# The first of equal maxima by a small bf16 product, one slot later, and weight conversions placed anew

## The chip, the cores and the metric

The kernel runs on one core of a Trainium2 chip. The metric is device time in microseconds for one execution, the median of eight: 1227.68 us (1223.66 to 1229.91). Five engines work side by side, each through its own instructions in order: TensorE (PE; its weight loads are PEld), VectorE (DVE), ScalarE (ACT), GpSimd (POOL) and SyncE (SP), whose queue issues most of the transfers.

## The reference: clustered attention, then a gated feed-forward layer

```python
# q, k, v: (4, 8, 768, 64) f32; centroids (8, 16, 64) f32
q_assign = argmax(q_n @ c_n.T)        # cluster of each query, first of equal maxima
k_assign = argmax(k_n @ c_n.T)        # cluster of each key
mask = q_assign[:, :, :, None] == k_assign[:, :, None, :]
scores = where(mask, q @ k.T / 8, -1e9)
scores = scores - max(scores)
attn = exp(scores) / (sum(exp(scores)) + 1e-9)
x = (attn @ v) -> (3072, 512)         # heads side by side
h = x @ w_in                          # w_in (512, 2048), float64
out = (h * erf(softplus(h))) @ w_out  # w_out (2048, 512), float64
```

A query attends only to the keys of its own cluster. Where no key has it, all scores are equal.

## The kernel before

**Pairs and units.** A pair `p` is two heads of one batch; there are 16, four to a batch. For each pair there are 12 units: two halves of 384 queries times six blocks `j` of 128 keys. For one unit, `scores` multiplies k and q in f32 (`products`, one product for each head `e`) and adds a bf16 product of `km` and `qm`; ScalarE takes the exponential into `pr`; `accumulate` lets POOL sum `pr` over the blocks; `attend` multiplies `pr` with v into `av`. After six units `divide` sums over partitions (`psum`, TensorE), takes the reciprocal by a logarithm and an exponential (`inv`, ScalarE), refines it (`den`, VectorE) and writes the quotient `xT` (VectorE). `divide` is in two parts: the first issues `psum` and `inv`, the second the rest.

**Routing of a pair.** `qm` and `km` (bf16, in `lows`) hold for each head the other head's vectors and, in 32 more rows, one-hot clusters: 1 for a query's own cluster, and for a key 0 at its cluster and at most -2^60 elsewhere. Their product is 0 within a cluster and hugely negative without. `route(p)` makes them, with a `yield` between its steps: (1) load and transposition of q and k on VectorE; (2) the product with the centroids (`psim`) on TensorE and the casts of q's vectors on ScalarE (`vectors("q")`); (3) transposition out of PSUM (`sims`), first maximum over 16 clusters (`mx`) and comparison with it; (4) the casts of k's vectors on ScalarE; (5) the choice of the first of equal maxima: the comparison's 0 or 1 times a descending `rank`, a second maximum `mr`, then two comparisons (equality for the queries' 64 partitions, a difference for the keys') into `hot`, and its transposition `hotT`; (6) the conversion of `hotT` into `qm` and `km`: two pieces on VectorE, four and then two on ScalarE. `own` zeroes the rows of the other head.

**Maxima of a pair.** `shift(p)` is 24 products `sm` of `qm` and `km` with VectorE's maximum over each (`nmx`); after each half `nm`, a small transposition `pn` on TensorE, a copy `nmT` on ScalarE, and six transfers that put the maxima into a row of `qm`. Two `sm` make a step; the half's end (`nm`) and `pn` are steps too, 14 in all. `aside(p)` is `route` and then `shift`: 20 steps.

**Weights.** They come as float64 and are converted to f32 by integer work: per tile of 128x512, ScalarE's `split` (two instructions), three steps on VectorE (A: a lower bound, B: shift and mask, C: the sign and the rest) and one addition on POOL after C. C also issues the next tile's split, B issues a fetch on SP's queue. 32 tiles are 96 steps; `prepare(n)` runs `n` of them. Tiles wait in the space of `w_out` and in two halves of `a_s`.

**Order.** Batch 0 is a loop over 48 slots, one unit each, kept in the written order up to slot 44 (`FIRST` is 45). `plan` has one line for each slot `r` of a pair (r0 to r11): steps of the pair's own maxima, steps of the next pair's `aside` before and after the unit's scores, and conversion steps. The first part of `divide` runs at r2 and r8, before the steps "after"; the second part at r3 and r9. In slots 44 and 45 no conversions run. From slot 45 on, `pump` mixes in the feed-forward stream: `hp` (x times `w_in`), the gate on ScalarE (Softplus and Erf into `a_s`, each with a load of its function table) and POOL, and `po` (times `w_out`). From batch 1 on, units go in twos, five places to each, 30 to a pair; `ASIDE` lists the places at which a step of the next pair's `aside` runs, and a planner that works with its own estimates of cost is free to move instructions from there on, also ahead of earlier ones where nothing binds them.

**PSUM.** `ps_s` has two double buffers for `sc`. `ps_x` has four buffers that `psim`, `sm`, `pn`, `av`, `psum`, `hp` and `po` share: a product that starts in a buffer waits until the last reader of the tile before has done.

Most rows of the profile name line 58, since one helper records the instructions; they are told apart by the tiles. The functions in question:

Of the kernel before, what the change touches and what calls it, by code (L numbers as in the profile page):

```python
# [8 lines left out]
F32 = mybir.dt.float32  # L9
BF16 = mybir.dt.bfloat16  # L10
U32 = mybir.dt.uint32
I32 = mybir.dt.int32
ALU = mybir.AluOpType
ACT = mybir.ActivationFunctionType
AX = mybir.AxisListType
PSUM = bass.MemoryType.PSUM

P = 128
B, H, S, D = 4, 8, 768, 64
C = 16  # L20
NJ = S // P
Q = 32
NB = S // Q
HW = S // 2
# [11 lines left out]
BIG = 2.0**60  # L36
# [5 lines left out]
SLOTS = 5  # L42


ASIDE = (*range(5), 6, *range(8, 8 + 2 * NJ), 10 + 2 * NJ, 12 + 2 * NJ)
REST = 3
FIRST = 2 * NJ * HP - 3

# [18 lines left out]
def kernel(  # L67
# [20 lines left out]
    const = pool("const", 1)  # L88
# [3 lines left out]
    routep = pool("routep", 1)  # L92
# [7 lines left out]
    ps_x = pool("ps_x", 4, space=PSUM)  # L100
# [1 line left out]
    ident = const.tile([P, P], F32, name="ident")  # L102
    identb = const.tile([P, P], BF16, name="identb")
    minus = const.tile([P, D], F32, name="minus")
    rank = const.tile([P, C], F32, name="rank")
    ccT = const.tile([P, HP, 2 * C], F32, name="ccT")
    w_in = const.tile([P, DM // P, DFF], F32, name="w_in")
    w_out = const.tile([P, NFT, DM], F32, name="w_out")
# [52 lines left out]
            ge.memset(t["k"][e * D + SH : e * D + SH + 1, e], 1.0)  # L161
    for t in prs:
        ge.memset(t[:, :, HW : HW + 2], EPS)

# [105 lines left out]
    def route(p):  # L272
        st = pairs[p]
        low = lows[p % 2]
        for e in range(2 if p > 1 else 0):
            r = e * D + SH
            nc.sync.dma_start(out=low["q"][r : r + 1, e], in_=low["q"][r + 1 : r + 2, e])
        for nm in "qk":
            raw = rowp.tile([P, S], F32, name=nm + "T")
            ve.transpose(out=raw, in_=st.pop(nm).rearrange("p n t -> p (n t)"))  # L280
            st[nm + "T"], st[nm + "m"] = raw, low[nm]
        load_qk(p + 1)
        yield

        psim = ps_x.tile([P, HW], F32, name="psim", tag="x")
        for g in range(4):
            te.matmul(
                psim[2 * C * g : 2 * C * (g + 1)], lhsT=ccT[:, p % HP],
                rhs=st["qk"[g // 2] + "T"][:, (g % 2) * HW : (g % 2 + 1) * HW],
                start=True, stop=True,  # L290
            )

        def vectors(nm):
            for e in range(2):
                ae.copy(
                    out=low[nm][(1 - e) * D : (2 - e) * D, e], in_=st[nm + "T"][e * D : (e + 1) * D]
                )

        vectors("q")
        yield  # L300

        sims = routep.tile([P, HW], F32, name="sims")
        ve.transpose(out=sims, in_=psim)
        n = HW // C
        sim = sims.rearrange("p (g c) -> p g c", c=C)
        mx = routep.tile([P, n], F32, name="mx")
        ve.reduce_max(out=mx, in_=sim, axis=AX.X)
        ve.tensor_tensor(
            out=sim, in0=sim, in1=mx.unsqueeze(2).to_broadcast([P, n, C]), op=ALU.is_equal
        )  # L310
        yield
        vectors("k")
        yield

        ve.tensor_tensor(
            out=sim, in0=sim, in1=rank.unsqueeze(1).to_broadcast([P, n, C]), op=ALU.mult
        )
        mr = routep.tile([P, n], F32, name="mr")
        ve.reduce_max(out=mr, in_=sim, axis=AX.X)

        hot = routep.tile([P, HW], BF16, name="hot")
        for r, op in ((slice(0, D), ALU.is_equal), (slice(D, P), ALU.subtract)):
            ve.tensor_tensor(
                out=hot[r].rearrange("p (g c) -> p g c", c=C), in0=sim[r],
                in1=mr[r].unsqueeze(2).to_broadcast([D, n, C]), op=op,
            )
        hotT = routep.tile([P, HW], BF16, name="hotT")
        ve.transpose(out=hotT, in_=hot)
        yield
        late = []  # L330
        for half in range(2):
            cols = slice(half * HW, (half + 1) * HW)
            for e in range(2):
                r = slice(e * D, e * D + Q)
                g = slice(half * Q, (half + 1) * Q)
                if half == 0:
                    ve.tensor_scalar_mul(out=low["q"][r, e, cols], in0=hotT[g], scalar1=own[g, e : e + 1])
                else:
                    late.append((low["q"][r, e, cols], hotT[g], own[g, e : e + 1]))
                g = slice(D + half * Q, D + (half + 1) * Q)  # L340
                ae.copy(out=low["k"][r, e, cols], in_=hotT[g])
        for dst, src, scale in late:
            ae.activation(out=dst, in_=src, func=ACT.Copy, scale=scale)
        yield


# [249 lines left out]
    def aside(p):  # L596
# [3 lines left out]


    plan = (
        (1, 0, 1, 1), (1, 0, 2, 0), (1, 0, 2, 0), (1, 0, 1, 0), (0, 0, 0, 0), (0, 0, 2, 0),
        (0, 0, 2, 1), (0, 0, 2, 1), (0, 1, 0, 3), (0, 0, 0, 3), (0, 0, 2, 1), (0, 0, 1, 2),
    )
    ready = {0: aside(0)}
    part = iter(())
# [1 line left out]
    def advance(p, n):  # L609
        for _ in range(n):  # L610
            next(ready[p])
# [9 lines left out]
        )  # L621
    ve.tensor_copy(out=identb, in_=ident)
    ve.memset(minus, -1.0)
    for c in range(C):
        ve.memset(rank[0:D, c : c + 1], float(C - c))
    ve.tensor_scalar_mul(out=rank[D:P], in0=rank[0:D], scalar1=BIG)
    ve.memset(alleps, S * EPS)
    for t in maxima:
        ve.memset(t, FLOOR)
# [6 lines left out]
    advance(0, 1)  # L636
    products(0)
    products(1)
    advance(0, 4)
    prepare(2)  # L640
    advance(0, NJ + 1)
    prepare(1)
# [98 lines left out]
```

## Time and profile before

| | |
|---|---|
| median of eight executions | 1227.68 us |
| the profiled execution | 1226.05 us |
| its span, first to last instruction | 1224.2 us |
| busy: PE / DVE / ACT / POOL | 1157.0 / 540.0 / 567.8 / 464.8 us |
| mean granted TensorE clock | 0.987 |
| slots of batch 0, about | 31 to 195 us |
| transfers | 42.95 MB |

A row of a group has the engine, the operation, output and inputs, sizes and count; then busy us, mean ns of one, idle time before, and what ended that. In rows in order of time the first two numbers are start and duration in us. TensorE's f32 products appear as two records each. `w_out` in a VectorE or ScalarE row of batch 0 is mostly a weight tile in conversion, since the tiles wait in that space.

### The profile page before, as it was taken

The numbers are of one execution on the slowest core, as the hardware profiler recorded it, in microseconds if no ns is written. First come the engines' busy times: TensorE is split into PE (matmuls) and PEld (weight loads), VectorE is DVE, ScalarE is ACT, GpSimd is POOL, SyncE is SP. The second block draws the span as 40 slices with busy tenths as digits, with TensorE's granted clock in tenths as the row PEclk, the third lists the DMA queues.
The fourth block names the chain that finished last, engine by engine and source line by source line (L and its number), as shares of the span: only waits on it lengthen the run. The fifth ranks groups of instructions, "written<-read, shape, count | busy, mean of one in ns | idle before, by whom it ended". The sixth has DMA issues, their size and how long they took to land.

```text
span 1224.2 us, 13359 instructions
## 1 busy us (share of the span) xinstructions
PE 1157.0 (95%) x4897; PEld 617.5 (50%) x4897; DVE 540.0 (44%) x999; ACT 567.8 (46%) x675; POOL 464.8 (38%) x462
## 2 busy tenths in 40 slices
PE   4888879989999999999999999999999999999998
PEld 1222235554454445565455445556456456576663
DVE  6889885674444345334344345334435112011121
ACT  3656556658352637165364445356263254132222
POOL 2467764357332344144343244235234343030200
PEclk9999999899999999999999999999999999999999
DMA  7344323132020202010020201002000000000000
GB/s 134 80 102 103 83 83 84 42 104 40 9 48 9 48 1 40 9 35 13 14 44 1 48 10 27 22 10 39 9 22 1 9 9 1 17 1 17 1 18 18
DMA packets 140753, 42.95 MB, mean 35 GB/s; under 512 B 133520, under 2 KB 133520, under 8 KB 140688
## 3 DMA queue, kind: packets, MB, share of 16 engines
q1 hardware_dynamic: 137552, 41.70, 15.2%
q10 hardware_dynamic: 3136, 0.39, 0.3%
q8 instruction: 39, 0.64, 0.2%
q14 instruction: 26, 0.21, 0.1%
HBM read 35.68 MB, written 6.29 MB: 34 GB/s over the span
## 4 chain that ended last, share of the span: by engine, by line
PE 74%; DVE 11%; issue 7%; ACT 6%; DMA 2%; POOL 0%; SPq 0%; ACTq 0%; DVEq 0%
PE po L58 25%; PE hp L58 24%; PE sc L58 12%; PE av L58 7%; PE sm L58 4%; DVE nmx L58 3%; ACT L58 2%; DVE w_out L58 2%; DVE den L58 1%; ACT inv L58 1%; PE psim L58 1%; DVE sims L58 1%; PE psum L58 1%; ACT km L58 1%; ACT pr L58 1%
## 5 line engine op out<-in xcount | busy, mean ns | idle before, releaser
L58 PE MATMUL hp<-xT,w_in 128*128 128x256 f32 x1536 | 382.7, 386 | 3.3 <-DVE xT L58 2.4
L58 PE MATMUL po<-w_out,g 128*128 128x512 f32 x768 | 367.8, 597 | 0.6 <-DVE den L58 0.6
L58 POOL TENSOR_TENSOR acc<-acc,pr 128x384 f32<-128x384 f32 x256 | 239.6, 967 | 316.0 <-ACT pr L58 315.8
L58 PEld LDWEIGHTS hp<-xT,w_in 128*128 128x128 f32 x1536 | 286.1, 191 | 121.5 <-issue 79.8
L58 DVE TENSOR_REDUCE nmx<-sm 128x1 f32<-128x384 f32 x384 | 195.2, 550 | 145.2 <-PE sm L58 144.4
L58 ACT ACT_TABLE_LOAD x113 | 145.0, 1283 | 230.8 <-DVE g L58 128.8
L58 ACT ACTIVATE pr<-sc 128x768 f32<-128x768 f32 x192 | 147.4, 807 | 167.0 <-PE sc L58 161.4
L58 PEld LDWEIGHTS po<-w_out,g 128*128 128x128 f32 x768 | 141.8, 190 | 107.2 <-issue 94.4
L58 PE MATMUL sc<-qT,kT 64*128 64x384 f32 x768 | 186.0, 539 | 6.0 <-ACT pr L58 5.9
L58 POOL TENSOR_TENSOR g<-a_s,g 128x512 f32<-128x512 f32 x88 | 111.0, 1295 | 198.9 <-ACT a_s L58 198.9
L58 DVE COPY g<-hp 128x512 f32<-128x512 f32 x96 | 65.9, 687 | 257.3 <-PE hp L58 257.0
L58 PE MATMUL av<-pr,in_v 128*64 128x386 f32 x768 | 144.7, 505 | 2.9 <-DVE nmx L58 2.9
L58 PE MATMUL sm<-km,qm 128*128 128x384 bf16 x384 | 105.7, 341 | 28.8 <-DVE nmx L58 13.3
L58 PEld LDWEIGHTS sc<-qT,kT 64*128 64x128 f32 x768 | 71.2, 192 | 85.5 <-issue 44.0
L58 POOL TENSOR_TENSOR acc<-pr,pr 128x384 f32<-128x384 f32 x64 | 66.1, 1053 | 94.1 <-ACT pr L58 94.1
L58 PEld LDWEIGHTS av<-pr,in_v 128*64 128x64 f32 x768 | 49.9, 138 | 93.2 <-issue 78.1
L58 PEld LDWEIGHTS <-qm 128*128 128x128 bf16 x384 | 35.1, 99 | 99.0 <-issue 72.8
L58 DVE SCALAR_TENSOR_TENSOR den<-psum,inv 128x384 f32<-128x384 f32 x32 | 17.8, 557 | 144.1 <-ACT inv L58 143.6
L58 ACT ACTIVATE a_s<-a_s 128x2048 f32<-128x2048 f32 (+2 forms) x40 | 55.8, 1413 | 12.8 <-DMA a_s<-in_moe_w_out_dram 8.3
L58 ACT ACTIVATE a_s<-g 128x2048 f32<-128x2048 f32 x24 | 45.8, 1910 | 33.2 <-DVE g L58 31.8
L58 PE MATMUL sc<-qm,km 64*128 64x384 bf16 x384 | 59.4, 328 | 1.9 <-DMA qm<-nmT 1.9
L58 ACT COPY nmT<-pn 6x128 bf16<-6x128 bf16 x32 | 8.0, 252 | 99.4 <-PE pn L58 99.0
(66 smaller groups left out, 603.3 us busy)
## 6 DMA issues: line engine op xcount, KB each, us to landing
w_out<-in_moe_w_in_dram SPq DMA_DIRECT2D x16, 512.0 KB, 4.6
in_q<-in_q_dram SPq DMA_DIRECT2D x64, 96.0 KB, 3.0
in_v<-in_v_dram SPq DMA_DIRECT2D x32, 192.0 KB, 3.0
out_dram<-osb SPq DMA_DIRECT2D x24, 256.0 KB, 2.0
in_k<-in_k_dram SPq DMA_DIRECT2D x60, 96.0 KB, 3.3
a_s<-in_moe_w_out_dram SPq DMA_DIRECT2D x8, 512.0 KB, 3.5
w_out<-in_moe_w_out_dram SPq DMA_DIRECT2D x8, 512.0 KB, 4.1
qm<-nmT SPq DMA_DIRECT2D x192, 0.2 KB, 1.7
```

The source lines that it names most:

```text
L58: ins = getattr(self.engine, name)(*args, **kw)
```

## The change

The first of equal maxima is no longer chosen by rank and a second maximum on VectorE. The first comparison writes 0 or 1 as bf16 (`hot`), which is transposed at once (`hotT`, still step 3). In the last step TensorE multiplies it with a constant 128x128 matrix `first`: 1 on the diagonal, -1 from each earlier cluster of the same 16. The result `won` in PSUM is 1 for the first maximum and at most 0 elsewhere. The conversions read `won`: a query's is its product with `own`, not below 0 (VectorE, and ScalarE's Relu); a key's is `won` times 2^60 minus 2^60 (ScalarE). `first` is built by POOL at the start, and the 17 instructions for `rank` go.

`route` has five steps now, `aside` 19. In batch 0, step 3 with the transposition stays at r1, k's vectors stay at r2, and the product with the conversions stands in r4, after that slot's scores (before: conversions in r3). The maxima of the next pair's first half end at r8 and r9 (before: r7 and r8). The conversion steps of a pair are 0, 0, 1, 0, 2, 2, 1, 1, 2, 0, 1, 2 over its slots (before: 1, 0, 0, 0, 0, 0, 1, 1, 3, 3, 1, 2): twelve in both, and since slots 44 and 45 have none, the last pair of the batch now runs ten rather than six. From batch 1 on, place 6 leaves `ASIDE`: the product and the conversions stand at place 4, where the second maximum stood.

```diff
@@ -42,7 +42,7 @@
 SLOTS = 5
 
 
-ASIDE = (*range(5), 6, *range(8, 8 + 2 * NJ), 10 + 2 * NJ, 12 + 2 * NJ)
+ASIDE = (*range(5), *range(8, 8 + 2 * NJ), 10 + 2 * NJ, 12 + 2 * NJ)
 REST = 3
 FIRST = 2 * NJ * HP - 3
 
@@ -102,7 +102,8 @@
     ident = const.tile([P, P], F32, name="ident")
     identb = const.tile([P, P], BF16, name="identb")
     minus = const.tile([P, D], F32, name="minus")
-    rank = const.tile([P, C], F32, name="rank")
+    first = const.tile([P, P], BF16, name="first")
+    nbig = const.tile([P, 1], F32, name="nbig")
     ccT = const.tile([P, HP, 2 * C], F32, name="ccT")
     w_in = const.tile([P, DM // P, DFF], F32, name="w_in")
     w_out = const.tile([P, NFT, DM], F32, name="w_out")
@@ -161,6 +162,17 @@
             ge.memset(t["k"][e * D + SH : e * D + SH + 1, e], 1.0)
     for t in prs:
         ge.memset(t[:, :, HW : HW + 2], EPS)
+
+    ge.memset(first, -1.0)
+    for base, pattern, sign, op, fill in (
+        (-1, [[1, P]], -1, ALU.is_ge, 0.0),
+        (0, [[-C, P // C], [0, C]], 1, ALU.is_ge, 0.0),
+        (0, [[-1, P]], 1, ALU.not_equal, 1.0),
+    ):
+        ge.affine_select(
+            out=first, in_=first, compare_op=op, fill=fill, base=base, pattern=pattern,
+            channel_multiplier=sign,
+        )
 
 
 
@@ -305,42 +317,38 @@
         sim = sims.rearrange("p (g c) -> p g c", c=C)
         mx = routep.tile([P, n], F32, name="mx")
         ve.reduce_max(out=mx, in_=sim, axis=AX.X)
+        hot = routep.tile([P, HW], BF16, name="hot")
         ve.tensor_tensor(
-            out=sim, in0=sim, in1=mx.unsqueeze(2).to_broadcast([P, n, C]), op=ALU.is_equal
+            out=hot.rearrange("p (g c) -> p g c", c=C), in0=sim,
+            in1=mx.unsqueeze(2).to_broadcast([P, n, C]), op=ALU.is_equal,
         )
+        hotT = routep.tile([P, HW], BF16, name="hotT")
+        ve.transpose(out=hotT, in_=hot)
         yield
         vectors("k")
         yield
 
-        ve.tensor_tensor(
-            out=sim, in0=sim, in1=rank.unsqueeze(1).to_broadcast([P, n, C]), op=ALU.mult
-        )
-        mr = routep.tile([P, n], F32, name="mr")
-        ve.reduce_max(out=mr, in_=sim, axis=AX.X)
-
-        hot = routep.tile([P, HW], BF16, name="hot")
-        for r, op in ((slice(0, D), ALU.is_equal), (slice(D, P), ALU.subtract)):
-            ve.tensor_tensor(
-                out=hot[r].rearrange("p (g c) -> p g c", c=C), in0=sim[r],
-                in1=mr[r].unsqueeze(2).to_broadcast([D, n, C]), op=op,
-            )
-        hotT = routep.tile([P, HW], BF16, name="hotT")
-        ve.transpose(out=hotT, in_=hot)
-        yield
-        late = []
+        won = ps_x.tile([P, HW], F32, name="won", tag="x")
+        te.matmul(won, lhsT=first, rhs=hotT, start=True, stop=True)
+
         for half in range(2):
             cols = slice(half * HW, (half + 1) * HW)
             for e in range(2):
                 r = slice(e * D, e * D + Q)
                 g = slice(half * Q, (half + 1) * Q)
                 if half == 0:
-                    ve.tensor_scalar_mul(out=low["q"][r, e, cols], in0=hotT[g], scalar1=own[g, e : e + 1])
+                    ve.tensor_scalar(
+                        out=low["q"][r, e, cols], in0=won[g], scalar1=own[g, e : e + 1], scalar2=0.0,
+                        op0=ALU.mult, op1=ALU.max,
+                    )
                 else:
-                    late.append((low["q"][r, e, cols], hotT[g], own[g, e : e + 1]))
+                    ae.activation(
+                        out=low["q"][r, e, cols], in_=won[g], func=ACT.Relu, scale=own[g, e : e + 1]
+                    )
                 g = slice(D + half * Q, D + (half + 1) * Q)
-                ae.copy(out=low["k"][r, e, cols], in_=hotT[g])
-        for dst, src, scale in late:
-            ae.activation(out=dst, in_=src, func=ACT.Copy, scale=scale)
+                ae.activation(
+                    out=low["k"][r, e, cols], in_=won[g], func=ACT.Identity, bias=nbig[g], scale=BIG
+                )
         yield
 
 
@@ -600,8 +608,8 @@
 
 
     plan = (
-        (1, 0, 1, 1), (1, 0, 2, 0), (1, 0, 2, 0), (1, 0, 1, 0), (0, 0, 0, 0), (0, 0, 2, 0),
-        (0, 0, 2, 1), (0, 0, 2, 1), (0, 1, 0, 3), (0, 0, 0, 3), (0, 0, 2, 1), (0, 0, 1, 2),
+        (1, 0, 1, 0), (1, 0, 2, 0), (1, 0, 1, 1), (1, 0, 0, 0), (0, 0, 1, 2), (0, 0, 1, 2),
+        (0, 0, 2, 1), (0, 0, 2, 1), (0, 1, 0, 2), (0, 1, 0, 0), (0, 0, 2, 1), (0, 0, 1, 2),
     )
     ready = {0: aside(0)}
     part = iter(())
@@ -621,9 +629,7 @@
         )
     ve.tensor_copy(out=identb, in_=ident)
     ve.memset(minus, -1.0)
-    for c in range(C):
-        ve.memset(rank[0:D, c : c + 1], float(C - c))
-    ve.tensor_scalar_mul(out=rank[D:P], in0=rank[0:D], scalar1=BIG)
+    ve.memset(nbig, -BIG)
     ve.memset(alleps, S * EPS)
     for t in maxima:
         ve.memset(t, FLOOR)
@@ -636,7 +642,7 @@
     advance(0, 1)
     products(0)
     products(1)
-    advance(0, 4)
+    advance(0, 3)
     prepare(2)
     advance(0, NJ + 1)
     prepare(1)
```

## The prediction

> **What bounds the kernel now.** I read, in this order, the busy table by stage, the order of work on ScalarE in the first batch, the same stretch on all engines, the waits, and the groups by shape. The busy table has, for each stretch, its length, then busy time and count on PE, PEld, DVE, ACT and POOL, the granted clock, the DMA share and GB/s.
>
> ```profile
> 40.00:60.00 20.00, 17.16 (x94) 5.83 (x93) 16.27 (x29) 15.13 (x26) 10.50 (x11) 1.00 0.28 74
> ...
> 100.00:120.00 20.00, 18.78 (x94) 5.76 (x93) 17.71 (x32) 11.75 (x19) 16.17 (x16) 0.91 0.52 115
> 120.00:140.00 20.00, 15.38 (x76) 5.19 (x77) 17.45 (x33) 11.37 (x18) 11.28 (x11) 0.96 0.31 91
> ...
> 600.00:700.00 100.00, 100.00 (x443) 54.75 (x442) 40.16 (x73) 49.60 (x59) 36.95 (x38) 1.00 0.17 32
> ```
>
> There are two regimes. From 20 to 180 us (batch 0) VectorE is busy 81 to 90% of each 20 us and TensorE 72 to 94%; neither is full, so the written order matters. From 300 to 1200 us TensorE is busy 99% (its gaps sum to 9.5 us) and VectorE at most 47% of each 100. A saving on VectorE can count only in the first regime; a microsecond on TensorE's queue counts in full in the second.
>
> The next lines are ScalarE's rows from slot r9 of pair 2 to r0 of pair 3, with start, duration and what ended the idle time:
>
> ```profile
> 133.71 0.79 ACT L58 ACTIVATE pr<-sc 128x768 f32<-128x768 f32 x1
> ...
> 135.54 0.80 ACT L58 ACTIVATE pr<-sc 128x768 f32<-128x768 f32 x1
> 141.52 0.67 ACT L58 ACTIVATE w_out<-w_out 128x512 f32<-128x512 f32 x1 [5.19 <-DMA w_out<-in_moe_w_in_dram]
> 142.10 0.80 ACT L58 ACTIVATE pr<-sc 128x768 f32<-128x768 f32 x1
> ...
> 144.50 0.81 ACT L58 ACTIVATE pr<-sc 128x768 f32<-128x768 f32 x1
> ```
>
> One exponential per slot is the kernel's pulse. From r10 to r11 it stops for 6.56 us (135.54 to 142.10). The same gap is 60.80 to 67.16 (6.36) in pair 0 and 98.32 to 104.39 (6.07) in pair 1. Slots with the same four maxima, r6 to r7, take 3.02 (123.95 to 126.97). Three pairs in a row repeat every 37.24 us (the second pulse at 34.72, 71.98, 109.22, 146.46). Around the gap:
>
> ```profile
> 129.53 0.92 PE L58 MATMUL sc<-qT,kT 64*128 64x384 f32 x4
> ...
> 134.95 1.59 DVE L58 TENSOR_SCALAR w_out<-w_out 128x512 f32<-128x512 f32 x2
> ...
> 136.58 0.69 DVE L58 SCALAR_TENSOR_TENSOR w_in<-w_out 128x512 uint32<-128x512 uint32 x1
> 137.19 1.94 DVE L58 TENSOR_REDUCE nmx<-sm 128x1 f32<-128x384 f32 x4
> ...
> 137.79 0.32 PE L58 MATMUL sm<-km,qm 128*128 128x384 bf16 x1 [2.32 <-DVE nmx L58]
> ...
> 139.30 1.65 PE L58 MATMUL sc<-qT,kT 64*128 64x384 f32 x4
> ```
>
> VectorE works off the conversion steps of r8 and r9 (3+3) and the division before it reaches the maxima; TensorE stands 2.32 us at the fourth `sm`, which needs a free PSUM buffer; then its products run at half speed for a while (1.65 against 0.92 for four `sc`). In pair 2 ScalarE waits at the same place for the weights' DMA, in pair 1 for POOL's sums. All of these hang on the same bunch of conversions.
>
> Costs by shape (busy us, mean ns):
>
> ```profile
> L58 ACT COPY km<-hotT 32x384 bf16<-32x384 bf16 x64 | 32.5, 508 | 34.9 <-DVE hotT L58 33.7
> ...
> L58 DVE TENSOR_TENSOR hot<-sims,mr 64x384 bf16<-64x384 f32 x32 | 21.7, 679 | 0.7
> ...
> L58 ACT ACTIVATE inv<-psum,alleps 128x384 f32<-128x384 f32 x32 | 18.6, 581 | 30.9 <-PE psum L58 30.5
> ...
> L58 DVE TENSOR_TENSOR sims<-sims,rank 128x384 f32<-128x384 f32 x16 | 12.8, 798 | 0.3
> ...
> L58 DVE TENSOR_REDUCE mr<-sims 128x24 f32<-128x384 f32 x16 | 8.8, 550 | 0.4
> ```
>
> **The change, part by part.** The sum is made against the profiled execution, 1226.05 us (span 1224.2), which is 1.6 below the median 1227.68.
>
> *Removed from VectorE.* Per pair the multiplication by `rank` (0.798), the second maximum (0.550) and two comparisons (2 x 0.679): 2.71 us, with the 17 setup instructions (0.42 in the prologue, beside TensorE's first products). The first comparison now writes bf16; its nearest row is itself, 0.728, no change.
>
> *q's and k's conversions read PSUM.* No row shows a 32x384 read of PSUM on either engine. VectorE's: between 0.31 (shortest `qm<-hotT`) and 0.60 (its mean, beside POOL); I take 0.56, the 128x384 `den<-psum` row, since that is the same free size from PSUM. ScalarE's: between 0.508 (`km<-hotT`) and 0.613 (`qm<-hotT`); I take 0.58, the `inv<-psum` row, which reads PSUM with a bias. Six of them are 3.5 us against 3.35 before. In the instruction order VectorE's second conversion now waits for ScalarE's first, and ScalarE's second for VectorE's second: the engines alternate on `won`. VectorE loses one ScalarE conversion, about 0.65 with its handover; between 0 (ScalarE free and early) and 1.5 (an 0.81 exponential before it). Queued behind on VectorE are the two conversion steps of r4, then the maxima.
> [...]
>
> *Pairs 0 to 2.* I follow one period, from the pulse at 107.00. Up to r3 nothing moves: `hotT` (0.58) enters r1, and the conversion step that stood in r0 (0.81) leaves, so `nm` and the transposition of maxima come at 114.3 as before. In r4 ScalarE is free for the exponential at 117.6 (before: 121.20, behind the conversions), then the alternating conversions occupy it from about 118.5 to 122.8 and the weights' split to 124.1, so r5's exponential is at about 124.1 (before 121.98), r7's at 127.4 (126.97), r8's at 130.8 (130.71), r9's and r10's as before. So the saving on VectorE is spent by r10 on the alternation and on the four steps that r4 and r5 gain. But r8 and r9 now hold two steps, not six, so the maxima of r10 start at about 135.7 instead of 137.19, TensorE does not stand 2.32 us nor fall to half speed, the DMA for the next tile has over 10 us, and r11's exponential comes 2.5 to 3 us after r10's: about 138.4 instead of 142.10. Gain 3.7 at best, 0 if r4 to r7 slip as much; I take 3.0 for each of three pairs: -9.0 (ends 0 and -11).
>
> *Pair 3.* No conversions stand in r8 and r9 there before, so that gap is missing. Its pulse from r3 to r4 is 155.23 to 161.85, 6.62, against 4.90 in pair 2, because maxima, `rank` product and ScalarE's conversions come one after another. Moving the conversions behind r4's exponential gives 0 to -3.5; four more conversion steps (about 0.75 each) are written into this pair, though they are then missing right behind it, where VectorE's conversions stand on the chain as well. I take -1.5.
>
> *Prologue.* The chain on VectorE shortens by 2.34 (13.61 to 15.95), but TensorE's eight `sc` records occupy it until 14.61, and the alternation makes ScalarE finish at about 19.8 instead of 19.94; VectorE's next step waits for ScalarE's split behind that. I take -0.2 (0 to -1.5). POOL builds `first` after 7.67 in about 1.1 us (a memset 0.21 and three selects of 0.30), ready before 14.6.
>
> *k's vectors ahead.* The casts (2 x 0.83) keep their slot behind the division's logarithm and exponential; they pass no DMA. Costs nothing; cover is ScalarE's idle time, some 40% there. SP's queue sees the first half's maxima one slot later in pairs 0 to 3 (r9 for r8): six DMAs, 3.7 to 4.3 us, must land before the next r0, some 9 us on. Nothing.
>
> *won on TensorE.* 16 bf16 matmuls of 128x384. Each is like one `sm`: two between other matmuls move the next start by 0.33, so 0.16 each. Five lie in batch 0, where TensorE has gaps; 11 x 0.16 = +1.8 (ends 1.8 and, at 0.34 each, 3.7). Does it wait for `hotT`? VectorE's chain from psim is 0.58 + 0.55 + 0.73 + 0.58, 2.5 with handovers. In the order, three to eleven `hp` (0.43 a product) or `po` (0.86) stand between psim and won, 2.6 to 5.6 us. So 0, at worst 0.7 (an `osb` copy) in two pairs.
>
> *won's PSUM buffer.* It is one of four shared with `hp`, `po`, `sm`, `av`, `psum`. Pairs 6 to 15 matter. In four of these ten `psum` needs won's buffer, after `av` (4.04) and one `sc` (0.35), 4.6 us after won starts. The release takes won 0.4, q 0.56, k 0.61, q 0.56 and five more on ScalarE at 0.61: 5.2, or 5.9 behind a `g` copy. Wait 0.6 to 1.3. In five others it is a `hp` 7 us or more on, with a 1.28 table load and a 1.91 Erf inserted in ScalarE's conversions in three of them: release at about 8.5, wait 0 to 1. I take 4 x 1.0 + 0.5 = +4.5; at least 0; at worst a whole table load and gate activation (3.2) late in each of the first four, +12.
>
> Sum: -9.0 - 1.5 - 0.2 + 1.8 + 4.5 = -4.4, so 1221.6 for this execution and **1223.2** for the median.
>
> On the half-speed stretch: the row is `sc` at 1.65 after the 2.32 us stand, 0.92 otherwise; about 1 us of each pair's gap is this. [...]
>
> **Rivals.**
> *B, the alternation sets the pace.* If the backlog of ScalarE in r4 to r6 delays everything behind it by the 3 us that r10 gains, the period stays 37.24 and only the costs remain: 1227.7 + 1.8 + 4.5, 1234. For it: my own walk has r7 0.5 late. Against: ScalarE is busy only 11.37 of 20 us there.
> *C, won's buffer becomes TensorE's wait.* This ends slower. ScalarE must read won six times in order, and in several pairs a softplus and an Erf with their table loads (2 x 3.19) stand in front. It decides from a mean of (10.7 - 1.8) / 10 = 0.9 us over ten pairs; at 2 us each the time is 1223.2 + 15.5, 1239; at 1.3, 1232. Against: `psum` is held through ScalarE in the same way now, and the waits listed for TensorE above 300 us have one of 2.7 and none else over 1.
> *D, they cancel:* gains of 2 per pair against 6 to 7 of cost: 1226 to 1229.
>
> **How the numbers follow.** Forecast (faster) 0.60, D 0.15, B 0.13, C 0.12. What a measurement can tell from no change is 0.2%, 2.5 us: faster below 1225.2. The range: the best ends (-11 - 3.5 - 1.5 + 1.8) would give 1213.5; above, B's 1234 and the cheaper C lie inside, the dear C outside: 1214 to 1235. The forecast's own range is 1214 to 1225.
>
> **What would show it.** Right: period in batch 0 near 34 us, no 6 us gap from r10 to r11; r5's exponential later than now relative to r3; TensorE's gaps above 300 us grown by some 4 us, named for k's or q's rows on ScalarE; `hot` once per pair. Wrong: a period still at 37, a new gap at r4 to r6, or TensorE waits of 2 us and more behind `av`.

## The result and the profile after

The changed kernel takes 1234.27 us (median; 1232.67 to 1242.51), the kernel before beside it 1227.29. The ratio is 1.0069, with a 95% interval of 1.0055 to 1.0083: the change makes the kernel 0.7% slower. The forecast was 1223.2 and faster. Its profiled execution took 1234.43 us, with a span of 1232.7 us; below, its trace is read beside that of the kernel before.

To find where the time went I follow TensorE's *lead*. Each kind of matmul is counted at one fixed length (0.215 us for a `hp`, 0.43 for a `po`, and so on, the distance of two starts in an unbroken row). The lead is the difference between the times at which the two traces have the same sum of this work behind them, after minus before, so a negative number is time gained. `won` counts as nothing, so its own work appears in the lead as a loss. It is worked out from the starts of TensorE's rows, and each figure comes from one execution.

| stretch of the changed kernel | forecast, us | lead at its end, us | change, us |
|---|---|---|---|
| prologue and batch 0, to 200 us | -10.7 | -6.6 | -6.6 |
| transition, 200 to 340 us | 0 | -3.2 | +3.4 |
| batches 1 to 3, 340 to 960 us | +6.3 | +8.5 | +11.7 |
| to the end | 0 | +8.3 | -0.2 |

The last row of the forecast has little to do: pair 15, the last that is routed, has its `won` at 916.8 us.

The busy table of the changed kernel, with the columns of the one of before:

```profile
40.00:60.00 20.00, 16.09 (x78) 5.33 (x78) 12.92 (x26) 12.12 (x20) 10.10 (x10) 0.91 0.42 125
100.00:120.00 20.00, 19.28 (x108) 6.01 (x102) 17.52 (x35) 13.41 (x21) 14.17 (x15) 1.00 0.39 78
120.00:140.00 20.00, 16.63 (x90) 5.66 (x89) 17.51 (x31) 12.80 (x21) 15.30 (x15) 1.00 0.36 99
600.00:700.00 100.00, 99.69 (x435) 54.48 (x433) 36.91 (x68) 49.18 (x60) 37.91 (x38) 1.00 0.15 28
```

From 40 to 60 us TensorE does less than before (78 matmuls for 94), from 100 to 140 more (198 for 170). So the first pair gains nothing and the later ones do. From 600 to 700 us TensorE was full before and has lost 8 matmuls of 443.

Costs by shape in the changed kernel (busy us, mean ns, then idle time ahead and what ended it):

```profile
L58 ACT ACTIVATE km<-won,nbig 32x384 bf16<-32x384 f32 x64 | 36.7, 573 | 33.8 <-DVE qm L58 33.0
...
L58 DVE TENSOR_SCALAR qm<-won,own 32x384 bf16<-32x384 f32 x32 | 19.4, 607 | 29.0 <-PE won L58 17.4 <-ACT km L58 11.5
L58 ACT ACTIVATE inv<-psum,alleps 128x384 f32<-128x384 f32 x32 | 18.6, 581 | 36.9 <-PE psum L58 36.6
L58 ACT ACTIVATE qm<-won,own 32x384 bf16<-32x384 f32 x32 | 18.3, 573 | 0.5
L58 DVE TENSOR_TENSOR hot<-sims,mx 128x384 bf16<-128x384 f32 x16 | 11.2, 700 | 0.5
...
L58 PE MATMUL won<-hotT,first 128*128 128x384 bf16 x16 | 5.3, 329 | 0.7 <-DVE hotT L58 0.5
```

ScalarE's conversions take 0.573 (taken: 0.58), VectorE's 0.607 (taken: 0.56, upper bound 0.60). `won` waits 0.5 us in all for `hotT`. The prices of the operations were nearly right; the new waits are in the idle column: ScalarE stood 33.0 us for VectorE's `qm`, VectorE 11.5 us for ScalarE's `km`. The two take turns on `won`.

ScalarE's rows for the gap that the forecast wanted closed, r9 of pair 2 to r1 of pair 3:

```profile
133.65 0.80 ACT L58 ACTIVATE pr<-sc 128x768 f32<-128x768 f32 x1
134.90 0.81 ACT L58 ACTIVATE pr<-sc 128x768 f32<-128x768 f32 x1 [0.46 <-PE sc L58]
137.98 0.81 ACT L58 ACTIVATE pr<-sc 128x768 f32<-128x768 f32 x1 [2.26 <-PE sc L58]
...
140.65 0.81 ACT L58 ACTIVATE pr<-sc 128x768 f32<-128x768 f32 x1 [0.74 <-PE sc L58]
142.86 0.81 ACT L58 ACTIVATE pr<-sc 128x768 f32<-128x768 f32 x1 [1.40 <-PE sc L58]
```

From r10 to r11 it is 3.08 us (134.90 to 137.98) where it was 6.56; in pairs 0 and 1 it is 4.12 and 3.16 where it was 6.36 and 6.07. This gap is closed. From r4 to r5 it is now 6.3 us for 0.71, but from r3 to r4 0.78 for 4.91, since the conversions only stand on the other side of r4's exponential: from r3 to r6 pairs 1 and 2 take 7.8 us, for 7.7 before. What is new stands from r6 to r7: 5.12, 4.86 and 3.51 us in pairs 0, 1 and 2, about 3.0 before. The rows of all engines in pair 1 of the changed kernel, r4 to r7:

```profile
81.54 0.57 ACT L58 ACTIVATE km<-won,nbig 32x384 bf16<-32x384 f32 x1
82.15 0.61 DVE L58 TENSOR_SCALAR qm<-won,own 32x384 bf16<-32x384 f32 x1 [0.64 <-ACT km L58]
82.79 0.57 ACT L58 ACTIVATE km<-won,nbig 32x384 bf16<-32x384 f32 x1 [0.68 <-DVE qm L58]
...
85.76 1.24 ACT L58 ACTIVATE w_out<-w_out 128x512 f32<-128x512 f32 x2
86.47 2.02 DVE L58 TENSOR_SCALAR w_out<-w_out 128x512 f32<-128x512 f32 x2 [1.59 <-ACT w_out L58]
88.41 1.94 DVE L58 TENSOR_REDUCE nmx<-sm 128x1 f32<-128x384 f32 x4
...
89.00 0.32 PE L58 MATMUL sm<-km,qm 128*128 128x384 bf16 x1 [2.73 <-DVE nmx L58]
...
90.53 1.65 PE L58 MATMUL sc<-qT,kT 64*128 64x384 f32 x4
```

Read it from the bottom. TensorE stands 2.73 us for maxima; VectorE takes these only after its conversion step of r5; that step waited 1.59 us for ScalarE's split of the weights; the split stands behind six conversions of `won`. It is the old chain in a new place, with the half-speed products (1.65) at its end. In pair 2 the stand is the same, but the products behind it run at full speed:

```profile
124.79 0.32 PE L58 MATMUL sm<-km,qm 128*128 128x384 bf16 x1 [2.73 <-DVE nmx L58]
...
125.84 0.92 PE L58 MATMUL sc<-qT,kT 64*128 64x384 f32 x4
```

In batch 1 and later the changed rows are at the division. ScalarE in pair 10 of the kernel before, and then of the changed kernel:

```profile
557.69 1.28 ACT L58 ACT_TABLE_LOAD   x1
558.99 0.58 ACT L58 ACTIVATE inv<-psum,alleps 128x384 f32<-128x384 f32 x1
559.59 0.51 ACT L58 COPY km<-hotT 32x384 bf16<-32x384 bf16 x1
```

```profile
557.65 0.57 ACT L58 ACTIVATE km<-won,nbig 32x384 bf16<-32x384 f32 x1
...
559.99 0.57 ACT L58 ACTIVATE km<-won,nbig 32x384 bf16<-32x384 f32 x1
560.58 1.28 ACT L58 ACT_TABLE_LOAD   x1
561.88 0.58 ACT L58 ACTIVATE inv<-psum,alleps 128x384 f32<-128x384 f32 x1
```

Five conversions (557.65 to 560.56) now stand ahead of the logarithm `inv`, which starts 2.89 us later. TensorE behind it, in the changed kernel:

```profile
564.73 0.33 PE L58 MATMUL sm<-km,qm 128*128 128x384 bf16 x1
565.64 0.32 PE L58 MATMUL sm<-km,qm 128*128 128x384 bf16 x1 [0.58 <-DVE den L58]
567.02 0.70 PE L58 MATMUL hp<-xT,w_in 128*128 128x256 f32 x2 [1.06 <-DVE xT L58]
```

The PSUM buffers of `psum` and `av` come free only when VectorE has made `den` and `xT` from `inv`. Pairs 10 and 14 lose 2.1 us each in this way. In pairs 7, 9, 12 and 13 `psum` comes later, since it needs won's buffer. That is seen as a broken row, not as a wait: in pair 7, `psum` and eight `sc` and four short products took 2.56 us before (358.28 to 360.84); now two `sc` come ahead of `psum` and the row falls into 2, 5 and 1, together 3.58 us (355.38 to 358.96). The kernel before, and then the changed one:

```profile
358.28 0.82 PE L58 MATMUL psum<-acc,minus 128*64 128x384 f32 x4
```

```profile
355.38 0.91 PE L58 MATMUL sc<-qT,kT 64*128 64x384 f32 x2
356.36 0.87 PE L58 MATMUL psum<-acc,minus 128*64 128x384 f32 x4
```

### The profile page after: what moved, and what is told of

Read it like the earlier page. It is cut to its first block, busy times and chain, and to the rows that moved or that the text cites. A ratio compares the mean times of both kernels' runs of the same rounds, so it can differ in the third digit from the quotient of the medians.

```text
span 1232.7 us, 13307 instructions
## 1 busy us (share of the span) xinstructions
PE 1161.1 (94%) x4913; PEld 621.1 (50%) x4913; DVE 498.6 (40%) x919; ACT 567.1 (46%) x673; POOL 464.3 (38%) x466
## 4 chain that ended last, share of the span: by engine, by line
PE 64%; issue 6%; ACT 5%; DVE 3%; POOL 1%; DMA 1%; ACTq 0%; SPq 0%; DVEq 0%
PE po L58 25%; PE hp L58 21%; PE sc L58 10%; PE av L58 5%; PE sm L58 3%; ACT L58 2%; ACT a_s L58 1%; PE psum L58 1%; ACT inv L58 1%; DVE den L58 1%; PE psim L58 1%; ACT km L58 1%; ACT pr L58 0%; POOL g L58 0%; DVE xT L58 0%
## 5 line engine op out<-in xcount | busy, mean ns | idle before, releaser
L58 PE MATMUL hp<-xT,w_in 128*128 128x256 f32 x1536 | 387.8, 389 | 8.4 <-DVE xT L58 4.8
L58 PEld LDWEIGHTS <-qm 128*128 128x128 bf16 x384 | 35.3, 99 | 95.6 <-issue 83.6
L58 ACT ACTIVATE km<-won,nbig 32x384 bf16<-32x384 f32 x64 | 36.7, 573 | 33.8 <-DVE qm L58 33.0
```

The lines of the kernel that those rows point to most:

```text
L58: ins = getattr(self.engine, name)(*args, **kw)
```

## The experiments

Medians are of runs on the chip beside the kernel before, which took 1226.3 to 1227.8 us there. The lead is read at three points, in the profiled execution of each kernel:

| kernel | at 200 | at 340 | at 960 | loss 340 to 960 | median | ratio to before (95%) |
|---|---|---|---|---|---|---|
| changed | -6.6 | -3.2 | +8.5 | 11.7 | 1234.27 | 1.0069 (1.0055 to 1.0083) |
| e1_place6 | -4.4 | -7.4 | +3.6 | 11.0 | 1231.50 | 1.0039 (1.0020 to 1.0059) |
| e2_copied | -6.2 | -5.7 | +6.4 | 12.1 | 1234.03 | 1.0053 (1.0031 to 1.0075) |
| e3_spread_alone | -7.9 | -3.9 | -3.2 | 0.7 | 1222.76 | 0.9966 (0.9945 to 0.9986) |
| e4_product_bunched | -1.7 | -4.9 | +8.3 | 13.2 | 1236.46 | 1.0077 (1.0047 to 1.0106) |
| e5_copied_place6 | -2.9 | -9.5 | +0.9 | 10.4 | 1227.12 | 1.0004 (0.9985 to 1.0023) |
| e6_copied_all_place6 | -5.2 | -12.6 | -2.4 | 10.2 | 1226.79 | 1.0007 (0.9986 to 1.0028) |
| e7_won_r3 | -6.8 | -5.5 | +9.5 | 15.0 | 1235.42 | 1.0068 (1.0043 to 1.0093) |
| e8_copied_all_place6_r3 | -9.3 | -14.9 | -1.9 | 13.0 | 1223.79 | 0.9967 (0.9945 to 0.9988) |
| e9_steady | -6.4 | -5.5 | -4.2 | 1.3 | 1222.25 | 0.9957 (0.9941 to 0.9972) |
| e10_split_nocopy | -4.6 | -6.8 | +2.7 | 9.5 | 1229.60 | 1.0016 (1.0000 to 1.0032) |
| e11_steps_r3 | -10.3 | -8.3 | +3.5 | 11.8 | 1228.58 | 1.0004 (0.9984 to 1.0023) |
| e12_steady_steps | -12.3 | -13.0 | -11.3 | 1.7 | 1215.17 | 0.9898 (0.9879 to 0.9917) |

Six of these kernels have the same batch 0 (changed, e1, e2, e5, e9, e10); their leads at 200 us run from -2.9 to -6.6. The loss from 340 to 960 us has its spread too: the four kernels with the changed kernel's program from batch 1 on (changed, e4, e7, e11) lose 11.7 to 15.0, the three with e5's (e5, e6, e8) 10.2 to 13.0, the two with e9's (e9, e12) 1.3 and 1.7. A difference of 2 to 3 us in either column alone says nothing.

**Is it the place of `won` ahead of the division?**

```
-ASIDE = (*range(5), *range(8, 8 + 2 * NJ), ...)
+ASIDE = (*range(4), 6, *range(8, 8 + 2 * NJ), ...)
```

> Only the place of won and of the conversions in batches 1 to 3 is changed: from ahead of the division's logarithm back to behind it, two places later. Theory P (the place: won's buffer is wanted by psum while ScalarE still reads it, and inv comes behind six conversions): the 11.7 us that the changed kernel loses between 300 and 950 us shrink to the product's own work (9 x 0.16 = 1.4) and at most 2 more, so 1224 to 1227 us; batch 0 keeps its 6.6 us of lead at 200 us. Rival H (a PSUM buffer held through ScalarE costs wherever it stands): hp or sm wait in place of psum, and the time stays at 1232 to 1236.

1231.50, just under the rival's range, and 11.0 us are still lost from 340 to 960 us. Theory P falls; the rival's picture, a wait in another place, is there. Pair 10 of this kernel:

```profile
558.23 0.33 PE L58 MATMUL won<-hotT,first 128*128 128x384 bf16 x1
...
560.03 0.60 DVE L58 TENSOR_SCALAR qm<-won,own 32x384 bf16<-32x384 f32 x1
560.66 0.57 ACT L58 ACTIVATE km<-won,nbig 32x384 bf16<-32x384 f32 x1 [2.26 <-DVE qm L58]
...
562.53 0.32 PE L58 MATMUL sm<-km,qm 128*128 128x384 bf16 x1 [0.93 <-ACT km L58]
```

`won` is done at 558.6, but VectorE has the division and a `g` copy to do first and reads it at 560.03. ScalarE, which was free, waits 2.26 us for its turn, and then the first `sm` rows wait for k: 5.7 us over nine waits between 300 and 960 us.

**Is it the holding of won's buffer?** Pairs above HP = 4 are those that are routed in batches 1 to 3; `sims` is free by then.

```
         te.matmul(won, lhsT=first, rhs=hotT, start=True, stop=True)
+        if p > HP:
+            ve.tensor_copy(out=sims, in_=won)
+            won = sims
```

> In batches 1 to 3 VectorE copies won to SBUF at once, and the six conversions read the copy; the place stays that of the changed kernel. Theory P1 (psum waits for won's buffer): the steps of 1.1 to 2.3 us at pairs 7, 9, 12 and 13, 5.9 us in all, go, and those of 2.1 each at pairs 10 and 14 (inv behind the conversions on ScalarE) stay: 1228 to 1230. Theory P2 (it is the place on ScalarE in every pair): no gain, 1233 to 1236. Both wrong if it falls below 1227.

1234.03: no gain in time, as P2 said, but not for its reason alone. The trace shows what P1 expected of pairs 7, 9, 12 and 13: none of them loses more than 0.3 us at its `psum` any more. Pairs 10 and 14 now lose 3.8 and 5.5 instead of 2.1 each. The stands there are nearly those of the changed kernel (0.81 and 1.06 us in pair 10, for 0.58 and 1.06), but this time the clock fell behind them:

```profile
560.00:562.00 2.00, 0.93 (x3) 0.30 (x2) 1.96 (x5) 0.07 (x1) 2.00 (x3) 1.00 0.00 0
562.00:564.00 2.00, 2.00 (x4) 0.79 (x4) 0.87 (x2) 0.00 (x0) 1.05 (x2) 0.64 0.00 0
564.00:566.00 2.00, 2.00 (x6) 0.54 (x6) 0.45 (x1) 0.00 (x0) 0.00 (x0) 0.51 0.00 0
```

The granted clock, a mean over the stretch, is the third number from the end. Summed over 340 to 960 us, in stretches of 2 us, the clock that is missing from 1.00 comes to 8.5 us here, against 1.7 in the kernel before and 3.4 in the changed one. So up to 5.1 of e2's 12.1 us can be clock; its median is that of the changed kernel all the same.

**Which half of batch 0's change works, the spread or the shorter chain?** In the kernel before, only the steps per slot are replaced (e3); in the changed kernel they are put back (e4):

```
e3, on the kernel before:    1 0 0 0 0 0 1 1 3 3 1 2  ->  0 0 1 0 2 2 1 1 2 0 1 2
e4, on the changed kernel:   0 0 1 0 2 2 1 1 2 0 1 2  ->  1 0 0 0 0 0 1 1 3 3 1 2
```

> The kernel before with the conversion steps per slot of the changed one (0 0 1 0 2 2 1 1 2 0 1 2 for 1 0 0 0 0 0 1 1 3 3 1 2) and nothing else. Theory S (the bunch of six steps in r8 and r9 made the gap of 6 us there; the gap from r6 to r7 of the changed kernel is made by its six conversions on ScalarE standing in r4, ahead of the weights' split): here they stand in r3, so neither gap is left whole, the period falls to 34.5 to 36 us and the time to 1219 to 1224. Rival M (four more steps in r4 and r5 are what makes the gap from r6 to r7): it appears here too, the period stays at 37 and the time at 1226 to 1230.

> The changed kernel with the conversion steps per slot of the kernel before. Theory S: 2.7 us less of VectorE's work per pair does not reach the end, since the six steps of r8 and r9 still stand ahead of the maxima; the gap from r10 to r11 stays at 5 to 6 us, no lead at 200 us, and the time is 1238 to 1242 (1234.3 plus the 6.6 of lead lost, less up to 3 of what the spread costs in the transition). Rival V (VectorE's load alone sets the period): period 34.5 to 35.5, 1230 to 1235.

Theory S holds in the main in both, in e4 a little under its range of time. The spread alone gives periods of 34.6, 35.1 and 35.3 us, gaps from r6 to r7 of 3.1 to 3.6 and from r10 to r11 of 3.1 to 3.7, and 1222.76. The shorter chain on VectorE without it gives periods of 36.6, 35.0 and 37.3, gaps from r10 to r11 of 6.5, 4.7 and 6.4, and 1.7 us of lead at 200 us: 1236.46. So the gain of batch 0 came from the spread, and the 2.71 us taken off VectorE per pair by themselves bought little. In the transition e3 gives 4.0 of its 7.9 us back, which theory S did not say.

**The turns on `won`.** The copy and the place behind the division together (e5), and the copy in batch 0 too (e6: the same edit without its condition).

> Both edits in batches 1 to 3: won stands behind the division, and VectorE copies it to SBUF at once; batch 0 is that of the changed kernel. Theory A (VectorE and ScalarE taking turns on won's PSUM tile is what costs above 300 us: with the place alone, ScalarE stood idle 2.26 us at 558.4 for VectorE's first q and the next sm waited 0.93 for k, at nine pairs): the loss between 300 and 960 us falls from 11.5 to 1.5 to 3, and the time to 1222 to 1225. Rival K (the copy, 0.6 us on VectorE behind den, xT and g, takes the place of the turns): at least 1228.

> As the run before it, and the copy in batch 0 too. Theory A: the turns also lengthen ScalarE's row of conversions in r4 of batch 0 (some 0.65 to 1.5 per pair) and so the gap from r6 to r7: two to four us better than the run before it, 1219 to 1222, with gaps from r6 to r7 of 3.5 to 4.3 us. Rival L (it is the six conversions' own length and their place): within 1.5 us of the run before it, gaps as in the changed kernel, 4.2 to 5.

1227.12 and 1226.79. Theory A expected 1222 to 1225 from the first and falls: 10.4 us are still lost. Rival K's 1228 is not reached either. The turns are gone, and this line of the waits from 340 to 960 us in e5 has come instead:

```profile
PE sm L58 <- DVE qm L58: 5.2, 7, 2.0
```

At place 6 the copy and the two conversions on VectorE come so late that the first `sm`, two places on, waits for q. In batch 0 the copy changes nothing: the gaps from r6 to r7 are 5.5, 5.5 and 4.9, as rival L said.

**The place of `won` in batch 0:** r3, where the kernel before has the conversions (e7), and this with the copy and place 6 (e8).

```
-(1, 0, 1, 0), (1, 0, 2, 0), (1, 0, 1, 1), (1, 0, 0, 0), (0, 0, 1, 2), ...
+(1, 0, 1, 0), (1, 0, 2, 0), (1, 0, 1, 1), (1, 0, 1, 0), (0, 0, 0, 2), ...
```

> The changed kernel with won and its conversions in r3 of batch 0, where the kernel before has them, ahead of the division's second part and of r4's exponential; nothing else. Theory S (place): the gap from r6 to r7 falls to 3.0 to 3.5 us, that from r3 to r4 grows to about 5, the period is 34.5 to 35.5 us and the lead at 200 us 7 to 9; the losses above 300 us stay, so 1230 to 1234. Rival M (the conversions cost the same wherever they stand): the gap from r6 to r7 stays at 4.5 to 5, period 35.8, time 1233 to 1237.

> All three edits together: copy of won in every pair, behind the division in batches 1 to 3, in r3 in batch 0. If theories A and S both hold, 1217 to 1222, below both kernels and at or below the spread alone (1222.8). If the turns or the place are not the cause, 1224 or more.

e7 takes 1235.42, as rival M said, though not with its gaps: from r6 to r7 they fall to 3.7, 3.7 and 4.3, and from r3 to r4 they grow from 0.8 to 1.8 us to 5.0 to 5.3. The row of conversions costs about the same in front of r4's exponential as in front of the split, and the lead at 200 us (-6.8) is that of the changed kernel. e8, 1223.79, is just below what it was to be if a theory failed; its loss from 340 to 960 us, 13.0, says that one had.

**Neither place suits a step that both makes `won` and converts it.** So the step is parted: `won` and the copy at place 4, ahead of the division, the conversions at place 6, behind it (e9); and the same without the copy (e10).

```
         te.matmul(won, lhsT=first, rhs=hotT, start=True, stop=True)
+        if p > HP:
+            ve.tensor_copy(out=sims, in_=won)      # not in e10
+            won = sims                             # not in e10
+            yield
...
-ASIDE = (*range(5), *range(8, 8 + 2 * NJ), ...)
+ASIDE = (*range(5), 6, *range(8, 8 + 2 * NJ), ...)
```

> In batches 1 to 3 won and the copy to SBUF stay at place 4, ahead of the division, and the six conversions, from the copy, go back behind it, to place 6; batch 0 is that of the changed kernel. Theory N (neither place suits a step that both makes won and converts it: at place 4 the conversions stand ahead of inv, at place 6 they end too late for the first sm, which waited up to 2.0 us for k's or q's rows): the loss between 300 and 960 us falls from 10 to 13 in all forms so far to 1.5 to 4, and the time to 1222 to 1227. Rival O (the loss is the product itself, its weight load and its switch of form on TensorE, wherever it stands): the loss stays at 8 or more, 1230 to 1235.

> As the run before it without the copy: won at place 4, the conversions at place 6 read it in PSUM, so that its buffer is held two places longer. If the holding of a PSUM buffer is what TensorE waits for (the forecast's rival C), psum and hp wait some 3 us in most pairs and the time is 1240 to 1260. If only the conversions' place counts, it is within 2 us of the run before it.

e9 takes 1222.25. The loss from 340 to 960 us is 1.3, which is the product's own work (9 x 0.16 = 1.4): theory N holds. Its waits of TensorE over this stretch are nearly those of the kernel before; the longest:

```profile
PE sc L58 <- ACT pr L58: 3.6, 2, 2.7
PE pn L58 <- DVE nm L58: 1.3, 2, 0.9
PE sm L58 <- DVE osb L58: 0.8, 1, 0.8
```

Without the copy (e10) 9.5 us are lost. Both of that run's expectations fail: holding the buffer two places longer costs far less than 3 us a pair, but the conversions' place alone doesn't cure it either. Of the two edits, the copy and the conversions' place, neither leaves 11.7 us of loss (the changed kernel), the copy alone 12.1 (e2), the place alone 9.5 (e10), both 1.3 (e9). The copy takes away what is lost at the `psum` of pairs 7, 9, 12 and 13: e10 still loses 1.1, 1.1, 1.1 and 0.5 us there, as the changed kernel does. The place takes away the late `inv`, behind which e2 loses most of its time. That each edit alone buys so little comes of new losses, in e2 the clock, in e10 a stand of 1.99 us for `pr` in pair 8 with a fall of the clock behind it (0.50 from 422 to 424 us), and 1.3 us each in pairs 10 and 14, where `hp` waits for `den`.

**The gap from r6 to r7.** The two conversion steps of r4 are written in r3, so that the split stands ahead of the conversions on ScalarE (e11); and this together with e9 (e12).

```
-(1, 0, 1, 0), (1, 0, 2, 0), (1, 0, 1, 1), (1, 0, 0, 0), (0, 0, 1, 2), ...
+(1, 0, 1, 0), (1, 0, 2, 0), (1, 0, 1, 1), (1, 0, 0, 2), (0, 0, 1, 0), ...
```

> The changed kernel with the two conversion steps of r4 written in r3 (0 0 1 2 0 2 1 1 2 0 1 2), so that the weights' split stands ahead of the six conversions on ScalarE; nothing else. Theory Q (the gap from r6 to r7 comes of VectorE's step of r5 waiting 1.59 us for a split that stands behind the six conversions): that wait and TensorE's stand of 2.73 us go, the gap from r6 to r7 is 3.0 to 3.6 in every pair, the period 34 to 35, and the time 1228 to 1232. Rival R (ScalarE's row of 3.5 us of conversions delays the exponentials themselves): the gap stays above 4.2 and the time within 2 us of the changed kernel's 1234.

> The first and the third run of this set together. If theories N and Q both hold, 1216 to 1222, below both kernels and below the spread alone (1222.8). If either fails, 1224 or more.

e11 takes 1228.58, the gaps from r6 to r7 are 2.3, 3.0 and 2.6, the periods 35.9, 34.4 and 33.7. The time is that of theory Q, and its wait and its stand are gone; the gaps are a little shorter than it said, and two of the periods lie just outside its range. ScalarE, then VectorE in pair 1 of e11:

```profile
80.05 1.25 ACT L58 ACTIVATE w_out<-w_out 128x512 f32<-128x512 f32 x2
81.20 0.79 ACT L58 ACTIVATE pr<-sc 128x768 f32<-128x768 f32 x1
82.02 0.57 ACT L58 ACTIVATE km<-won,nbig 32x384 bf16<-32x384 f32 x1
```

```profile
84.72 2.09 DVE L58 TENSOR_SCALAR w_out<-w_out 128x512 f32<-128x512 f32 x2
```

The split (80.05) is done before the conversions begin, and VectorE's steps of r5 start with no wait where they waited 1.59.

e12 takes 1215.17, ratio 0.9898 (0.9879 to 0.9917): 1.0% below the kernel before, 0.6% below the spread alone and a little under the range expected. 12.3 us of lead at 200 us, 11.3 of them left at 960. The form of the selection that the change brought is no hindrance; its placing was. Whether the kernel before, with the spread and its split moved in the same way, would come as far was not run.

## Why the prediction was wrong

*Pairs 0 to 2, forecast -3.0 each.* The gap from r10 to r11 shrank by 2.2, 2.9 and 3.5 us, as the step said, and pair 2 went as it was walked through: r7 at 127.02 (said 127.4), r8 130.50 (130.8), r11 137.98 (138.4), a period of 34.17. Pairs 0 and 1 had 37.62 and 35.80, so the three gained -0.4, 1.4 and 3.1, together 4.1 of 9.0. The step that failed is the walk from r5 to r7, with "r9's and r10's as before" behind it and taken for all three pairs. It put the weights' split to 124.1 but did not ask who waits for the split. VectorE's next step did, and behind it stood the maxima of r6 and TensorE, 2.73 us, for a PSUM buffer. That stand is in pair 2 too, where the walk came out right; what pair 1 lost against pair 2 is mostly the clock. In the changed kernel the granted clock is 0.50 for 3.41 us behind the stand in pairs 0 and 1 (from 51.98 and 89.52 us), with gaps of 5.12 and 4.86 us, and stays at 1.00 in pair 2, with 3.51. The four `sc` behind this stand (2.73 or 2.74 us) take 1.65 us in these two pairs and in pair 1 of e1 and of e9, which have the same batch 0; they take 0.92 in pair 2 of the changed kernel and of e9 and in pair 1 of e2. The walk had counted such half-speed products in r10's old gap, not that a new stand could bring them back. e11, which moves only the two conversion steps of r4 and with them the split, takes 5.7 us off the changed kernel's time. In pair 0 another 1.6 us were lost from r1 to r6; of this no run shows the whole cause.

*Pair 3, -1.5.* From its r1 to its r9, 28.87 before and 27.88 after: -1.0, right.

*Prologue, -0.2 (0 to -1.5).* Probably wrong in sign. ScalarE's conversions begin at 16.24 for 16.56 but take 4.2 us for 3.4 and end at 20.43 for 19.94; the taking of turns on `won` eats what VectorE saves. The first `pr` of r1 comes 0.54 later, but by that pulse kernels with one and the same prologue differ by more: 35.26 to 36.35 in the ten that have the changed one, 34.72 and 35.31 in the two that have the old (before, e3).

*The prices.* VectorE's conversion 0.607 for 0.56 (upper end 0.60), ScalarE's 0.573 for 0.58, `won`'s own work 0.16 (e9: 1.3 over nine pairs), `won` waiting for `hotT` 0.5 in all: nearly right.

*won's PSUM buffer, +4.5 (0 to +12).* Measured: 11.7 from 340 to 960 us, less 1.4 of own work, 10.3. The mechanism was named and its place too, but the term was mis-sized. The four `psum` of won's buffer cost 1.1, 1.1, 1.1 and 0.5, together 3.8 for the 4.0 taken. What was missing is that ScalarE does the conversions ahead of `inv`: the working counted how long `won` is held, and not who else stands in ScalarE's queue behind the six reads. Pairs 10 and 14 cost 2.1 each by this. A `hp` of pair 8 waited 0.9 for won's buffer, as the term of 0.5 had it. Another 1.7 us are clock: at 750 us the same three stands as before (0.28, 0.42 and 0.89 us) were followed by 22 `hp` in 6.70 us instead of 5.02. These make 10.6, of which 0.3 came back elsewhere. "Costs nothing" was said of k's vectors, and no row speaks against it; but the move of the conversions from place 6 to 4, past the division's logarithm on ScalarE, was in the diff and had no term of its own.

*The transition, no term.* 3.4 us of lead were lost from 200 to 340 us, in two stands of TensorE that the waits name `sm` behind `g` (4.26 at 239.78) and behind maxima (4.01 at 259.92). Both are also in e7 and e11 (4.1 to 4.3 us), which have the same program from batch 1 on and the same spread of steps and lose 1.3 and 2.0 here. e4, which has the steps per slot of before, has neither (2.3 the longest) and gains 3.2; e1, with the same batch 0 and the product at place 6, has neither (2.1) and gains 3.0; the spread alone (e3) loses 4.0, with a stand of 4.0 behind `den`. So the spread and the places after it both have a part; how was not parted further, and the cause of this loss stays open.

*The rivals.* C is nearest for batches 1 to 3: 10.3 over nine pairs is 1.1 us a pair, where 1.3 was priced 1232. But it named the buffer alone, and e2 and e10 show that the buffer and `inv`'s place each keep most of the loss when the other is mended. B said that the period stays at 37.24: pair 0 does (37.62), pair 1 does in part, pair 2 does not. That its 1234 is the measured time is chance, since batch 0 did gain 6.6 us. The measured time lies inside the stated range, 1214 to 1235, by the same chance: with 4.1 us less gained in batch 0, 3.4 lost in the transition and 5.4 more lost after it, the sum turned from -4.4 to +8.4.

*The clock.* The forecast saw half-speed products behind the stand of 2.32 us (`sc` at 1.65 for 0.92), and its sum has no term for them behind new stands. They came behind shorter ones as well: in means over 2 us the clock was 0.64 and 0.51 behind stands of at most 1.06 us (e2, from 562 us). More of this is in the last section.

## What to carry to other kernels

When work is taken off one engine and its remainder moved to another slot, list what stands in *every* queue behind the moved instructions, and follow each to its next consumer: here the weights' split in batch 0 and the division's logarithm later, both on ScalarE, neither touched by the diff. In batches 1 to 3 the PSUM tile that two engines read was best copied out at once and converted later, in two steps with their own places (1.3 us of loss); making and converting it in one step fitted neither place (10.2 to 15.0). And where two causes stand together, undoing them one at a time can show little: try the pair before giving a cause up.

## What the runs showed of the hardware

The same stand does not always cost the same. TensorE stood 2.73 us in pair 1 (86.27 to 89.00) and in pair 2 (122.06 to 124.79) of the changed kernel, behind the same rows. In its trace and in that of the kernel before, the record of the granted clock holds only 1.00 and 0.50, and its changes lie whole multiples of 3.41 us apart. The busy table of the changed kernel, cut in steps of that length that meet these changes:

```profile
86.11:89.52 3.41, 0.68 (x4) 0.20 (x4) 3.02 (x5) 3.38 (x6) 3.10 (x4) 1.00 0.68 200
89.52:92.94 3.42, 3.42 (x12) 0.94 (x9) 1.42 (x3) 0.46 (x2) 1.86 (x2) 0.50 0.24 50
...
120.24:123.66 3.42, 1.82 (x11) 0.74 (x10) 1.79 (x3) 3.33 (x7) 3.42 (x4) 1.00 0.81 198
123.66:127.07 3.41, 2.28 (x13) 0.75 (x13) 3.07 (x6) 1.82 (x4) 1.53 (x3) 1.00 0.17 71
```

In pair 1 the whole stand lies in one of these stretches, in which TensorE is busy 0.68 of 3.41 us (20%); the clock of the next is 0.50, and r7 came 4.86 us after r6. In pair 2 the stand is parted over two stretches, busy 53% and 67%; the clock stayed 1.00, and r7 came after 3.51. The same stand in pair 1 of two kernels with the same batch 0 was followed by four `sc` in 1.65 us in e9 and in 0.92 in e2. And after 750 us in the changed kernel the clock fell behind stands of at most 0.89:

```profile
752.00:754.00 2.00, 2.00 (x7) 1.56 (x6) 0.00 (x0) 0.48 (x1) 1.21 (x2) 0.50 0.02 0
754.00:756.00 2.00, 2.00 (x8) 1.71 (x7) 0.51 (x2) 0.00 (x0) 0.00 (x0) 0.72 0.27 42
```

The 22 `hp` behind those stands took 6.70 us, where the kernel before has 5.02 behind the same three. From 40 to 1190 us the two traces have the clock at 0.50 for 16 times, 15 of 3.41 us and one of 6.83, so about 1.7 us of clock for most. In the 3.41 us ahead of the fall TensorE's rows (their ends are modelled) fill 0 to 35% in 14 of the 16, and 47 and 62% in the other two, of which the second is the one at 750 us. Ten more such stretches are filled to 46 to 63%, and the clock stayed at 1.00 behind them. So in these two traces the length of a stand alone did not tell whether the clock falls: behind 2.73 us it fell in pair 1 and not in pair 2, and it fell behind 0.89. What parts the two at 47 and 62% from the ten was not shown.
